# Four layers on one core: layer 2's key-value sums in bursts on two column halves, in place of layer-norm aggregation on GpSimd

## The chip, the core and the metric

The kernel runs on one NeuronCore of a Trainium2 chip. Its engines run side by side and meet through semaphores: PE (TensorE, matrix products; weight loads are shown apart as PEld), DVE (VectorE), ACT (ScalarE), POOL (GpSimd) and SP (SyncE, which here issues DMAs). SBUF is the working memory of 128 partitions; PE writes its results to the eight banks of PSUM. The metric is the device time of one execution in microseconds, the median of the runs.

## What is computed

Two pairs of layers are applied to x of 2048 rows and 512 columns in bf16, each with a layer norm ahead and a residual sum behind. Layers 0 and 2 are linear attention with 32 heads of 16 columns and a Hedgehog feature map; layers 1 and 3 are a gated unit with 1376 hidden columns.

```python
def _A_ref(x, wqkv, w_phi, wo):
    q, k, v = qkv[0], qkv[1], qkv[2]               # 32 heads x 16
    pq = jnp.einsum("bhsd,hdf->bhsf", q, w_phi)
    pk = jnp.einsum("bhsd,hdf->bhsf", k, w_phi)
    phi_q = jnp.concatenate([_softmax(pq, axis=-1), _softmax(-pq, axis=-1)], axis=-1)
    phi_k = jnp.concatenate([_softmax(pk, axis=-1), _softmax(-pk, axis=-1)], axis=-1)
    kv = jnp.einsum("bhsf,bhsd->bhfd", phi_k, v)
    z  = jnp.einsum("bhsf->bhf", phi_k)
    num = jnp.einsum("bhqf,bhfd->bhqd", phi_q, kv)
    den = jnp.einsum("bhqf,bhf->bhq", phi_q, z)[..., None] + 1e-6
    o = num / den
    return (lambda x, *d: x.transpose(*d))(o, 0, 2, 1, 3).reshape(B, S, D) @ wo
...
x = x + _A_ref(_layernorm(x, axis=-1), A_wqkv, A_w_phi, A_wo)
x = x + _B_ref(_layernorm(x, axis=-1), B_W_gate, B_W_up, B_W_down)
x = x + _A_ref(_layernorm(x, axis=-1), A_wqkv, A_w_phi, A_wo)
x = x + _B_ref(_layernorm(x, axis=-1), B_W_gate, B_W_up, B_W_down)
```

The sum over all rows in `kv` and `z` separates the two halves of an attention layer: no output of the layer can be made before the last row's key has been summed.

## The kernel before

x is held in SBUF as 16 tiles of 128 rows (`NT`); four tiles make a slab (`NSLAB`). A column chunk (`NC`, 128 columns) holds eight heads.

Order. Each operation is recorded by `op` or `dma` with the resources that it reads and writes and a planned duration. A planner (`Program.schedule`) then makes the order of each engine's instructions: it runs list schedules over a model of the engines and keeps the one whose replay is shortest. `WINDOW` limits how far each engine may reach ahead. So a change of one operation can move others, and the order in which an engine gets its instructions is fixed when the program is built. DMAs are issued from SP, and a few from ACT.

Layer norm. `ln_stats` makes each tile's statistics with `bn_stats` on DVE (line 551) and, for most tiles, `bn_aggr` on DVE (line 553), then variance plus epsilon (`rv1`, line 558) and the power -1/2 (`rstd`, line 559) on POOL. For tiles 8 to 15 of layer 0, `aggr_pool` (lines 562 to 577) instead takes mean and variance from the two halves in `bn_stats`' output by small POOL operations, for four tiles at a time, and makes rstd and nmr (mean times -rstd) too. `ln` then applies the norm: with rstd and nmr for layer 0's tiles from 4 on, the even ones on DVE (line 592), the odd ones on ACT (line 590); in all other cases on DVE with mean and rstd (line 594). The result goes through a DMA transpose (or, for layer 0's tiles 0 to 3, through PE) into `yT`.

Keys and values. `kv_proj` (one tile) and `kv_pair` (two) make k and v on PE, both exponentials of k (`expk`) and the copy of v (`vsb`) on ACT. `vsb` holds, for each tile and chunk, 128 columns of v and two ones. `knorm` makes the softmax sums on DVE (`Zk`, line 629; their reciprocals `rZk`, line 631) and multiplies `expk` by them in place on POOL (line 634, "phik"); the last two tiles are shared between POOL and DVE. `kv_acc` (line 663) sums, for each tile, eight groups (two signs by four chunks) over the rows: a matmul with 128 stationary columns of `expk` and 129 moving columns of `vsb`, into banks 0 to 2 with three groups to a bank. `kv_fin` multiplies the banks by a block mask into `kvbd` (128 columns of values in an order of d by head, 8 of denominators, 8 of the mask itself, `GW` = 144 in all): lines 674 ("kvbd") and 679 ("kvden"), a pair for each bank.

Queries. `q_proj` makes q transposed, a slab at a time, with its exponentials on ACT (`expq`, line 693). `num` (line 706) multiplies a tile of `expq` by `kvbd`, copies the three banks out (`numcp`), forms the denominators (`zm`, `zd`, `zr`, `ab`), the scaled sum (`tsc`, `o`), transposes it by DMA and multiplies by `wo` (line 737).

Gated unit. `glu_up` (line 758) and `glu_down` (line 785) do the gate, up and down products; `mix` interleaves them with `num` of the layer before and with layer norm, keys and values of the layer after. At the change from layer 1 to layer 2 the order recorded is:

```python
mix(steps_B(tiles(2)), steps_N([14, 15]) + steps_K(0))
mix(steps_B(tiles(3)), steps_K(1) + steps_K(2) + [lambda: self.q_proj(0, mring, "A2")])
for t in range(12):
    self.kv_acc(t, "A2")
for f in steps_K(3):
    f()
for t in tiles(3):
    self.kv_acc(t, "A2")
self.kv_fin("A2")
```

Of the kernel before, what the change touches and what calls it, by code (L numbers as in the profile page):

```python
# [345 lines left out]
FP32 = mybir.dt.float32  # L346
# [4 lines left out]
P = 128  # L351
# [5 lines left out]
NG = 8  # L357
GW = 144
# [10 lines left out]
class Kernel:  # L369
# [27 lines left out]
    def alloc(self, E):  # L397
# [17 lines left out]
        sb("vsb", [NT, NC, 130])  # L415
        sb("expq", [NSLAB, NC, 2, 512])
        sb("kvbd", [NG, GW])
# [9 lines left out]
        sb("mask8t", [8])  # L427
        sb("phi_c", [NC, DH])
# [5 lines left out]
        sb("agg", [4, 3], FP32)  # L434
        sb("aggw", [2], FP32)
# [6 lines left out]
        sb("ab", [2, 64])  # L442
        self.ps = E(nc.psum_tensor("ps", [P, 8, 512], FP32))
# [4 lines left out]
    def setup(self):  # L448
# [46 lines left out]
        op("pool", lambda e: e.memset(k.aggw[:, 0:1], -0.5), [], [r("aggw")], 100, "agg w0")  # L495
        op("pool", lambda e: e.memset(k.aggw[:, 1:2], 1.0 / D), [], [r("aggw")], 100, "agg w1")
        op("pool", lambda e: e.memset(k.vsb[:, :, :, 128:130], 1.0), [], [r("vones")], 250, "v ones")
        op("pool", lambda e: e.tensor_copy(k.kvbd[:, :, 136:144], k.mask8[:].unsqueeze(1).to_broadcast([P, NG, 8])), [r("mask8")], [r("kvones")], 230, "kv ones")
# [33 lines left out]
    def late_weights(self):  # L532
        dma, r, k = self.dma, self.r, self
        pieces = []
        wo_v = self.A_wo.rearrange("(c h d) n -> h d c n", c=4, h=8)
        for h in range(8):
            pieces.append((lambda h: lambda rd: dma("sp", lambda e: e.dma_start(k.wo_p[h:128:8, :, :], wo_v[h]), [rd], [r("wo", h)], 65536, f"dma wo{h}"))(h))
# [9 lines left out]
    def ln_stats(self, ts, tag):  # L547
        op, r, k = self.op, self.r, self
        t0, t1 = ts[0], ts[-1] + 1
        for t in ts:  # L550
            op("dve", (lambda t: lambda e: e.bn_stats(k.stats6[:, t, :], k.x_sb[:, t, :]))(t), [r("x", t)], [r("st", t)], 685, f"{tag} stats {t}")  # L551
            if tag != "L0" or ts[0] < 8:
                op("dve", (lambda t: lambda e: e.bn_aggr(k.mv[:, t, :], k.stats6[:, t, :]))(t), [r("st", t)], [r("mv", t)], 172, f"{tag} aggr {t}")
        if tag == "L0" and ts[0] >= 8:
            return self.aggr_pool(ts, tag)
# [4 lines left out]


    def aggr_pool(self, ts, tag):
        op, r, k = self.op, self.r, self
        t0, t1 = ts[0], ts[-1] + 1
        n = t1 - t0
        s6 = k.stats6[:, t0:t1, :].rearrange("p t (u j) -> p t u j", u=2)
        RS, RV, RR = [r("st", t) for t in ts], [r("rv1", t) for t in ts], [r("rstd", t) for t in ts]
        sm, df = k.agg[:, 0:n, 0:2], k.agg[:, 0:n, 2:3]
        d = 225 + 4 * n
        op("pool", lambda e: e.tensor_tensor(df, s6[:, :, 0, 1:2], s6[:, :, 1, 1:2], ALU.subtract), RS, [r("agg", 1)], d, f"{tag} agdif {t0}")  # L570
        op("pool", lambda e: e.tensor_tensor(sm, s6[:, :, 0, 1:3], s6[:, :, 1, 1:3], ALU.add), RS, [r("agg", 0)], d, f"{tag} agsum {t0}")
        op("pool", lambda e: e.tensor_tensor(df, df, df, ALU.mult), [r("agg", 1)], [r("agg", 1)], d, f"{tag} agsq {t0}")
        op("pool", lambda e: e.tensor_tensor(sm, sm, k.aggw[:].unsqueeze(1).to_broadcast([P, n, 2]), ALU.mult), [r("agg", 0), r("aggw")], [r("agg", 0)], d, f"{tag} agmul {t0}")
        op("pool", lambda e: e.tensor_scalar(df, df, 0.25, EPS_LN, op0=ALU.mult, op1=ALU.add), [r("agg", 1)], [r("agg", 1)], d, f"{tag} agv {t0}")
        op("pool", lambda e: e.tensor_tensor(k.rv1[:, t0:t1, :], df, k.agg[:, 0:n, 1:2], ALU.add), [r("agg", 0), r("agg", 1)], RV, d, f"{tag} rv1 {t0}")
        op("pool", lambda e: e.tensor_tensor(k.rstd[:, t0:t1, :], k.rv1[:, t0:t1, :], k.mhalf[:, 0:n], ALU.pow), RV + [r("mhalf")], RR, 550 + 20 * n, f"{tag} rstd {t0}")  # L576
        op("pool", lambda e: e.tensor_tensor(k.nmr[:, t0:t1, :], k.agg[:, 0:n, 0:1], k.rstd[:, t0:t1, :], ALU.mult), [r("agg", 0)] + RR, [r("nmr", t) for t in ts], d, f"{tag} nmr {t0}")

    def ln(self, t, tag, on_act=False, pe_bank=None, stats=True, copy_act=False):
# [4 lines left out]
        if tag == "L0" and t > 3:  # L584
            if t < 8:
                op("pool", lambda e: e.tensor_scalar(k.nmr[:, t, :], k.mv[:, t, 0:1], k.rstd[:, t, :], -1.0, op0=ALU.mult, op1=ALU.mult), [r("mv", t), r("rstd", t)], [r("nmr", t)], 280, f"{tag} nmr {t}")
            how = ("dve", "act", "pool")[on_act]
            dep, dst = [r("x", t), r("nmr", t), r("rstd", t)], [r("yt", yb)]
            if how == "act":
                op("act", lambda e: e.activation(k.ytile[:, yb, :], k.x_sb[:, t, :], ACT.Identity, scale=k.rstd[:, t, :], bias=k.nmr[:, t, :]), dep, dst, 825, f"{tag} apply {t}")  # L590
            else:
                op(how, lambda e: e.tensor_scalar(k.ytile[:, yb, :], k.x_sb[:, t, :], k.rstd[:, t, :], k.nmr[:, t, :], op0=ALU.mult, op1=ALU.add), dep, dst, 407 if how == "dve" else 2090, f"{tag} apply {t}")
        else:
            op("dve", lambda e: e.tensor_scalar(k.ytile[:, yb, :], k.x_sb[:, t, :], k.mv[:, t, 0:1], k.rstd[:, t, :], op0=ALU.subtract, op1=ALU.mult),
               [r("x", t), r("mv", t), r("rstd", t)], [r("yt", yb)], 407, f"{tag} apply {t}")
# [16 lines left out]
    def kv_proj(self, t, ring, tag):  # L612
# [9 lines left out]
        op("act", lambda e: e.activation(k.vsb[:, t, :, 0:128], k.pb[bv][:].rearrange("p (c n) -> p c n", c=4), ACT.Copy),  # L622
# [18 lines left out]
    def kv_pair(self, t, ring, tag):  # L641
# [11 lines left out]
        op("act", lambda e: e.activation(k.vsb[:, t:t + 2, :, 0:128], k.ps[:, vb[0]:vb[0] + 2, :].rearrange("p b (c n) -> p b c n", c=4), ACT.Copy),  # L653
# [4 lines left out]
    def kv_acc(self, t, tag):  # L658
        op, r, k = self.op, self.r, self
        for g in range(NG):  # L660
# [3 lines left out]
                k.pb[bank][:, j * 130:j * 130 + 129], k.expk[:, t, s, c * 128:(c + 1) * 128], k.vsb[:, t, c, 0:129],  # L664
# [3 lines left out]
    def kv_fin(self, tag):  # L668
        op, r, k = self.op, self.r, self
        for bank in range(3):  # L670
            g0 = bank * 3
            n = min(3, NG - g0)
            pv = k.pb[bank][:, 0:n * 130].rearrange("p (g m) -> p g m", m=130)
            op("dve", (lambda g0, n, pv: lambda e: e.tensor_tensor(
                k.kvbd[:, g0:g0 + n, 0:128].rearrange("p g (d h) -> p g d h", h=8),
                pv[:, :, 0:128].rearrange("p g (h d) -> p g d h", h=8),
                k.mask8[:].unsqueeze(1).unsqueeze(1).to_broadcast([P, n, 16, 8]), ALU.mult))(g0, n, pv),
               [self.RP[bank], r("mask8")], [r("kvbd", bank)], 550 if n == 3 else 430, f"{tag} kvbd {bank}")
            op("dve", (lambda g0, n, pv: lambda e: e.scalar_tensor_tensor(
                k.kvbd[:, g0:g0 + n, 128:136], pv[:, :, 128:129].to_broadcast([P, n, 8]), 0.5 * EPS_DEN,  # L680
                k.mask8[:].unsqueeze(1).to_broadcast([P, n, 8]), ALU.add, ALU.mult))(g0, n, pv),
# [115 lines left out]
    def emit(self):  # L797
# [41 lines left out]
        for li in (0, 2):  # L839
# [51 lines left out]
            if not last:  # L891
                mix(steps_B(tiles(2)), steps_N([14, 15]) + steps_K(0))
                mix(steps_B(tiles(3)), steps_K(1) + steps_K(2) + [lambda: self.q_proj(0, mring, "A2")])
                for t in range(12):
                    self.kv_acc(t, "A2")
                for f in steps_K(3):
                    f()
                for t in tiles(3):
                    self.kv_acc(t, "A2")
# [72 lines left out]
```

## Time and profile before

| | us |
|---|---|
| median of 3 runs | 392.02 |
| lowest and highest run | 391.07, 392.33 |
| the profiled execution | 392.02 |
| its span from the first to the last instruction | 390.3 |

| part of the span | us | what PE does |
|---|---|---|
| layer 0's weights, norm, keys and sums | 0 to 53.7 | waits in part for the other engines |
| first `num` of layer 0 | 53.68 | |
| first gate product of layer 1 | 72.12 | from here nearly without gaps |
| last sums of layer 2 | 237.22 to 239.83 | |
| first `num` of layer 2 | 240.04 | |
| first gate product of layer 3 | 257.82 | |
| last matmul | 378.26 to 387.76 | `glu_down` of the last tiles |

The span is what one execution took from its first to its last instruction; the run's time is 1.7 us longer. A stretch's busy time is summed for each engine. In a list of instructions each line gives the start, the time, the engine, the line of the kernel, the operation with its output and input shapes, and how many equal ones were merged; a bracket gives the idle time ahead of it and who ended it. A matmul's own duration holds the time that it needs to pass through the array, so matmuls overlap; the distance from start to start is what each adds.

### The profile page before, as it was taken

What the parts mean: (1) busy time and instruction counts of PE and PEld (TensorE: products, weight loads), DVE (VectorE), ACT (ScalarE), POOL (GpSimd) and SP (SyncE); (2) the same over time, 40 slices, a digit from 0 to 9 for tenths busy, and PEclk for the clock granted to TensorE, in tenths of its full rate; (3) what the DMA queues carried; (4) which work ended last, traced back from release to release, by engine and by line L of the source; (5) the groups of instructions that cost most, each with busy time, mean ns of one, the idle gap of its engine ahead of it and who ended that gap; (6) DMA issues with size and microseconds to landing.
All of it is one profiled execution on the core that took longest, in us unless ns stands there. A gap on an engine that the chain in (4) does not pass through costs nothing.

```text
span 390.3 us, 6397 instructions
## 1 busy us (share of the span) xinstructions
PE 379.4 (97%) x2331; PEld 208.0 (53%) x2331; DVE 272.0 (70%) x547; ACT 206.6 (53%) x389; POOL 168.5 (43%) x284
## 2 busy tenths in 40 slices
PE   5999989999999999999999999999999999999997
PEld 3445554667644544444444457567774554444444
DVE  4999978877766888866766777897986776232222
ACT  5898859834633404533453484985563462553340
POOL 5499936641724363372244543584553242100000
DMA  6833682311311322401000110132323132100002
GB/s 179 228 67 71 191 299 53 69 40 32 53 40 27 43 55 44 84 10 28 14 15 0 27 29 3 40 80 57 55 55 69 27 42 67 29 14 27 17 12 67
DMA packets 61663, 23.01 MB, mean 59 GB/s; under 512 B 53472, under 2 KB 60608, under 8 KB 61632
## 3 DMA queue, kind: packets, MB, share of 16 engines
q1 hardware_dynamic: 60912, 22.02, 24.4%
q10 hardware_dynamic: 720, 0.59, 0.5%
q8 instruction: 18, 0.29, 0.3%
q14 instruction: 13, 0.11, 0.1%
HBM read 7.91 MB, written 2.10 MB: 26 GB/s over the span
## 4 chain that ended last, share of the span: by engine, by line
PE 88%; POOL 4%; ACT 3%; DMA 2%; DVE 1%; issue 1%; ACTq 0%; POOLq 0%
PE ps L758 39%; PE ps L785 19%; PE ps L617 7%; PE ps L737 7%; PE ps L690 6%; PE ps L706 4%; PE ps L663 3%; PE ps L648 2%; POOL expk L634 2%; ACT expq L693 2%; DVE stats L551 1%; DMA x_sb<-in_A_x_dram 1%; DMA hT<-in_A_wqkv_dram 1%; ACT expk L620 1%; POOL rstd L576 1%
## 5 line engine op out<-in xcount | busy, mean ns | idle before, releaser
L758 PE MATMUL ps<-yT,Wg 128*128 128x512 bf16 (+3 forms) x440 | 130.1, 337 | 0.5 <-DMA yT<-ytile 0.2
L758 PE MATMUL ps<-yT,Wu 128*128 128x512 bf16 (+3 forms) x440 | 129.6, 336 | 0.0
L760 ACT ACTIVATE gate_sb<-ps 128x512 bf16<-128x512 f32 (+3 forms) x110 | 55.9, 512 | 105.3 <-PE ps L758 102.9
L785 PE MATMUL ps<-Wd,hT 128*128 128x512 bf16 (+2 forms) x363 | 106.8, 373 | 0.0
L634 POOL TENSOR_TENSOR expk<-expk,rZk 128x1024 bf16<-128x1024 bf16 (+1 forms) x32 | 59.5, 1878 | 37.1 <-DVE rZk L631 19.7
L758 PEld LDWEIGHTS ps<-yT,Wg 128*128 128x128 bf16 (+1 forms) x440 | 43.4, 100 | 33.8 <-issue 1.1
L758 PEld LDWEIGHTS ps<-yT,Wu 128*128 128x128 bf16 (+1 forms) x440 | 43.7, 100 | 32.6 <-ACT expk L765 0.2
L767 DVE TENSOR_TENSOR hT<-gate_sb,expk 128x512 bf16<-128x512 bf16 (+3 forms) x73 | 29.8, 409 | 37.9 <-ACT expk L765 33.0
L785 PEld LDWEIGHTS ps<-Wd,hT 128*128 128x128 bf16 (+1 forms) x363 | 35.3, 98 | 36.6 <-DVE x_sb L787 0.6
L551 DVE BATCH_NORM_STATS2 stats<-x_sb 128x6 f32<-128x512 bf16 x64 | 42.6, 682 | 5.5 <-DMA x_sb<-in_A_x_dram 5.1
L366 ACT ACTIVATE numbf<-ps 128x432 bf16<-128x432 f32 x64 | 33.1, 536 | 19.5 <-PE ps L706 19.4
L629 DVE TENSOR_REDUCE Zk<-expk 128x64 f32<-128x1024 bf16 x32 | 37.7, 1194 | 5.7 <-ACT expk L620 5.4
L731 POOL TENSOR_TENSOR osb<-tsc 128x512 bf16<-128x512 bf16 x28 | 32.5, 1162 | 19.9 <-DVE tsc L726 17.8
L737 PE MATMUL ps<-wo_p,oT 128*128 128x512 bf16 x128 | 39.8, 379 | 0.0
L770 DVE TENSOR_TENSOR hT<-gate_sb,ps 128x512 bf16<-128x512 bf16 (+2 forms) x37 | 22.7, 613 | 20.8 <-PE ps L758 19.6
L693 ACT ACTIVATE expq<-ps 128x1024 bf16<-128x1024 f32 (+1 forms) x40 | 32.6, 861 | 7.3 <-PE ps L690 7.0
L765 ACT ACTIVATE expk<-ps 128x512 bf16<-128x512 f32 (+3 forms) x73 | 36.1, 497 | 0.1
L706 PE MATMUL ps<-kvbd,expq 128*128 128x144 bf16 x256 | 35.0, 226 | 0.5 <-ACT numbf L366 0.5
L620 ACT ACTIVATE expk<-ps 128x512 bf16<-128x512 f32 x44 | 23.9, 598 | 21.5 <-PE ps L617 21.2
L690 PE MATMUL ps<-yT,Wqp 128*128 128x512 bf16 x128 | 34.6, 379 | 0.6 <-ACT expq L693 0.5
L787 DVE TENSOR_TENSOR x_sb<-x_sb,ps 128x512 bf16<-128x512 bf16 (+1 forms) x33 | 22.0, 669 | 18.8 <-PE ps L785 18.4
L559 POOL TENSOR_TENSOR rstd<-rv,mhalf 128x1 f32<-128x1 f32 (+1 forms) x53 | 31.9, 607 | 2.9
(73 smaller groups left out, 429.2 us busy)
## 6 DMA issues: line engine op xcount, KB each, us to landing
out_dram<-x_sb SPq DMA_DIRECT2D x15, 128.0 KB, 1.7
x_sb<-in_A_x_dram SPq DMA_DIRECT2D x3, 512.0 KB, 6.2
Wu<-in_B_W_up_dram SPq DMA_DIRECT2D x4, 344.0 KB, 5.9
Wg<-in_B_W_gate_dram SPq DMA_DIRECT2D x4, 344.0 KB, 5.5
Wd<-in_B_W_down_dram SPq DMA_DIRECT2D x5, 256.0 KB, 6.9
yT<-ytile SPq DMA_TRANSPOSE x60, 2.5
hT<-in_A_wqkv_dram ACTq DMA_DIRECT2D x4, 128.0 KB, 3.1
x_sb<-in_A_x_dram SPq DMA_DIRECT2D x4, 128.0 KB, 3.7
```

What stands on the lines that cost most here:

```text
L366: return e.activation(out, in_, ACT.Copy) if hasattr(e, "activation") else e.tensor_copy(out, in_)
L551: op("dve", (lambda t: lambda e: e.bn_stats(k.stats6[:, t, :], k.x_sb[:, t, :]))(t), [r("x", t)], [r("st", t)], 685, f"{tag} stats {t}")
L629: op("dve", lambda e: e.tensor_reduce(k.Zk[:, zb, :], k.expk[:, t, :, :].rearrange("p s (h f) -> p (s h) f", f=16), AX.X, ALU.add), [r("ex ...
L634: op(eng, (lambda s0, s1: lambda e: e.tensor_tensor(k.expk[:, t, s0:s1, :].rearrange("p s (h f) -> p (s h) f", f=16), k.expk[:, t, s0:s1, ...
L690: op("pe", (lambda c, ic, bank: lambda e: e.matmul(k.pb[bank][:], k.Wqp[:, ic, c * 128:(c + 1) * 128], k.yT[:, ic, st * 512:(st + 1) * 512 ...
L693: op("act", (lambda c0, s, b0: lambda e: e.activation(k.expq[:, st, c0:c0 + w, s, :], k.ps[:, b0:b0 + w, :], ACT.Exp, scale=(1.0 - 2.0 * s ...
L706: op("pe", (lambda s, c, j, g0, bank: lambda e: e.matmul(k.pb[bank][:, j * GW:(j + 1) * GW], k.expq[:, st, c, s, tt * 128:(tt + 1) * 128], ...
L737: op("pe", (lambda c, bank: lambda e: e.matmul(k.pb[bank][:], k.oT[:, ob, c, :], k.wo_p[:, c, :], start=(c == 0), stop=(c == NC - 1)))(c, ...
L758: op("pe", (lambda bank, W, ic, fc, Mf: lambda e: e.matmul(k.pb[bank][0:Mf, 0:n], W[:, ic, fc * 128:fc * 128 + Mf], k.yT[:, ic, c0:c0 + n] ...
L760: op("act", (lambda Mf, gb, gs: lambda e: e.activation(k.gate_sb[0:Mf, gs, 0:n], k.pb[gb][0:Mf, 0:n], ACT.Relu))(Mf, gb, gs), [self.RP[gb] ...
L765: op("act", (lambda Mf, ub, tu: lambda e: e.activation(k.expk[0:Mf, tu, 0, 0:n], k.pb[ub][0:Mf, 0:n], ACT.Copy))(Mf, ub, tu), [self.RP[ub] ...
L785: op("pe", (lambda fc, Kf, u, c0, bank, m0, m1: lambda e: e.matmul(k.pb[bank][:, m0:m1], k.hT[0:Kf, u, c0:c0 + 128], k.Wd[0:Kf, fc, m0:m1] ...
```

## The change

Two things are exchanged. The first goes back to one way of aggregating statistics: `aggr_pool` and its tiles `agg` and `aggw` are gone, `bn_aggr` on DVE is done for all tiles, POOL makes `rv1` and `rstd`, `nmr` is made only for tiles whose norm ACT applies, and the even tiles of layer 0 are applied on DVE with mean and rstd, as all others are.

The second concerns the sums. `vsb`, `kvbd` and the layout of the sums are split into two halves of four heads each (`u`): 64 columns of values and their own ones, `GH` = 72 columns for each half of `kvbd`. The products in `num`'s tail (`zm`, `ab`, `tsc`) follow this layout, and so do the rows of `wo_p`. Layer 0 keeps `kv_acc`, with 130 moving columns in two runs of 65, and `kv_fin` with the new layout. Layer 2 uses `kv_burst` and `kv_burst_fin`: each group becomes two matmuls with 64 stationary columns and 65 moving columns, one for each half of heads, whose results go to partitions 0 to 63 and 64 to 127 of the same columns of one bank (bank 0 for one sign, bank 1 for the other). Four tiles are recorded as one operation of 64 matmuls; the last slab comes as a burst of three tiles and a burst of one. `kv_burst_fin` waits for the last burst, makes four masked products, adds epsilon to all denominators in one operation (`zt`) and spreads them with the mask in another (`kvden`, which writes all groups). Layer 2's q products of slab 0 are recorded behind the third slab's keys instead of inside the mixed list, with two banks to an exponential (banks 2 and 3).

```diff
-                mix(steps_B(tiles(3)), steps_K(1) + steps_K(2) + [lambda: self.q_proj(0, mring, "A2")])
-                for t in range(12):
-                    self.kv_acc(t, "A2")
+                mix(steps_B(tiles(3)), steps_K(1) + steps_K(2))
+                for ts in [[0, 1, 2, 3], [4, 5, 6, 7], [8, 9, 10, 11]]:
+                    self.kv_burst(ts, "A2")
                 for f in steps_K(3):
                     f()
-                for t in tiles(3):
-                    self.kv_acc(t, "A2")
-                self.kv_fin("A2")
+                self.q_proj(0, cycle([2, 3]), "A2", w=2)
+                for ts in [[12, 13, 14], [15]]:
+                    self.kv_burst(ts, "A2")
+                self.kv_burst_fin("A2")
...
+    def kv_burst(self, ts, tag):
+        r, k = self.r, self
+
+        def acc(e):
+            for t in ts:
+                for s in range(2):
+                    for c in range(NC):
+                        for u in range(2):
+                            last = e.matmul(
+                                k.pb[s][u * 64:u * 64 + 64, c * 65:c * 65 + 65], k.expk[:, t, s, c * 128 + u * 64:c * 128 + u * 64 + 64], k.vsb[:, t, c, u, 0:65],
+                                start=(t == 0 and c == 0), stop=(t == NT - 1), skip_group_check=True)
+            return last
+        self.op("pe", acc, [r("phik", t, s) for t in ts for s in range(2)] + [r("v", t) for t in ts] + [r("vones")], self.RP[0:2],
+                190 + 256 * len(ts), f"{tag} kvacc {ts[0]}")
+
+    def kv_burst_fin(self, tag):
+        op, r, k = self.op, self.r, self
+        m8 = k.mask8[:].rearrange("p (u h) -> p u h", u=2)
+        for s in range(2):
+            pv = k.pb[s][:, 0:260].rearrange("p (g m) -> p g m", m=65)
+            for u in range(2):
+                op("dve", (lambda s, u, pv: lambda e: e.tensor_tensor(
+                    k.kvbd[:, s * 4:s * 4 + 4, u, 0:64].rearrange("p g (d h) -> p g d h", h=4),
+                    pv[:, :, 0:64].rearrange("p g (h d) -> p g d h", h=4),
+                    m8[:, u, :].unsqueeze(1).unsqueeze(1).to_broadcast([P, 4, 16, 4]), ALU.mult))(s, u, pv),
+                   [self.RP[s], r("mask8")] + [r("kvbd", g) for g in range(s * 4, s * 4 + 4)] * u, [r("kvbd", g) for g in range(s * 4, s * 4 + 4)], 420, f"{tag} kvbd {s} {u}")
+        op("dve", lambda e: e.tensor_scalar(k.zt[:].rearrange("p (s g) -> p s g", s=2), k.ps[:, 0:2, 64:260:65], 0.5 * EPS_DEN, None, op0=ALU.add),
+           self.RP[0:2], [r("zt")], 160, f"{tag} zt")
+        op("dve", lambda e: e.tensor_tensor(
+            k.kvbd[:, :, :, 64:68], k.zt[:].unsqueeze(2).unsqueeze(3).to_broadcast([P, NG, 2, 4]),
+            m8.unsqueeze(1).to_broadcast([P, NG, 2, 4]), ALU.mult),
+           [r("zt"), r("mask8")], [r("kvbd", g) for g in range(NG)], 220, f"{tag} kvden")
...
-            if tag != "L0" or ts[0] < 8:
-                op("dve", (lambda t: lambda e: e.bn_aggr(k.mv[:, t, :], k.stats6[:, t, :]))(t), [r("st", t)], [r("mv", t)], 172, f"{tag} aggr {t}")
-        if tag == "L0" and ts[0] >= 8:
-            return self.aggr_pool(ts, tag)
+            op("dve", (lambda t: lambda e: e.bn_aggr(k.mv[:, t, :], k.stats6[:, t, :]))(t), [r("st", t)], [r("mv", t)], 172, f"{tag} aggr {t}")
...
-        if tag == "L0" and t > 3:
-            if t < 8:
-                op("pool", lambda e: e.tensor_scalar(k.nmr[:, t, :], k.mv[:, t, 0:1], k.rstd[:, t, :], -1.0, op0=ALU.mult, op1=ALU.mult), [r("mv", t), r("rstd", t)], [r("nmr", t)], 280, f"{tag} nmr {t}")
-            how = ("dve", "act", "pool")[on_act]
...
+        if on_act:
+            op("pool", lambda e: e.tensor_scalar(k.nmr[:, t, :], k.mv[:, t, 0:1], k.rstd[:, t, :], -1.0, op0=ALU.mult, op1=ALU.mult), [r("mv", t), r("rstd", t)], [r("nmr", t)], 280, f"{tag} nmr {t}")
...
+        row = lambda h: 64 * (h // 4) + h % 4
...
+            pieces.append((lambda h: lambda rd: dma("sp", lambda e: e.dma_start(k.wo_p[row(h):row(h) + 61:4, :, :], wo_v[h]), [rd], [r("wo", h)], 65536, f"dma wo{h}"))(h))
```

## The prediction

> **What bounds the kernel now.** I read the totals first, then the chain that ended last, then busy time by stretch, then the instruction order of the two stretches that the change touches.
>
> ```profile
> PE 379.4 (97%) x2331; PEld 208.0 (53%) x2331; DVE 272.0 (70%) x547; ACT 206.6 (53%) x389; POOL 168.5 (43%) x284
> PE 88%; POOL 4%; ACT 3%; DMA 2%; DVE 1%; issue 1%; ACTq 0%; POOLq 0%
> 20.00:40.00 20.00, 19.69 (x136) 10.50 (x135) 20.00 (x26) 18.11 (x23) 19.75 (x19) 1.00 0.32 67
> 222.00:240.00 18.00, 18.00 (x179) 12.16 (x178) 12.54 (x21) 10.26 (x19) 8.41 (x8) 1.00 0.11 23
> 240.00:260.00 20.00, 19.57 (x136) 10.86 (x136) 17.06 (x43) 18.01 (x28) 10.51 (x22) 1.00 0.23 47
> ```
>
> The columns after a stretch are busy us of PE, weight loads, DVE, ACT and POOL, then the granted clock (1.00 everywhere). From 72 us on PE has almost no gap, so whatever moves the head (0 to 54 us) or the change of layers (222 to 240 us) arrives at the end nearly whole. In the head PE is covered by DVE (20.00 of 20) and POOL (19.75): there the last of the sixteen phik products on POOL sets the end. In 222 to 240 PE itself is full.
>
> ```profile
> 23.06 0.31 DVE L592 TENSOR_SCALAR ytile<-x_sb,rstd,nmr 128x512 bf16<-128x512 bf16 x1
> ...
> 26.41 1.92 DVE L592 TENSOR_SCALAR ytile<-x_sb,rstd,nmr 128x512 bf16<-128x512 bf16 x1
> 28.25 0.54 DVE L631 RECIPROCAL rZk<-Zk 128x64 f32<-128x64 f32 x1
> ```
> ```profile
> 26.25 25.75 POOL L634 TENSOR_TENSOR expk<-expk,rZk 128x1024 bf16<-128x1024 bf16 x14
> ```
>
> POOL runs phik 2 to 15 without a gap from 26.25 to 52.0, 1.88 us a step. The same layer-norm apply takes DVE 0.31 us while POOL does small work, and 1.92 us when it arrives just after POOL has begun a phik: it ends as that phik ends (26.30 + 1.88 = 28.2).
>
> ```profile
> 234.14 1.47 PE L663 MATMUL ps<-vsb,expk 128*128 128x129 bf16 x23
> ...
> 237.22 2.77 PE L663 MATMUL ps<-vsb,expk 128*128 128x129 bf16 x45
> 239.83 0.38 PE L690 MATMUL ps<-yT,Wqp 128*128 128x512 bf16 x1
> 240.04 0.54 PE L706 MATMUL ps<-kvbd,expq 128*128 128x144 bf16 x6
> ```
> ```profile
> 238.70 1.08 DVE L674 TENSOR_TENSOR kvbd<-ps,mask 128x384 bf16<-128x384 f32 x2 [1.43 <-PE ps L663]
> 239.70 0.30 DVE L679 SCALAR_TENSOR_TENSOR kvbd<-ps,mask 128x24 bf16<-128x24 f32 x2
> ```
>
> Forty-five sums in 239.83 - 237.22 = 2.61 us: 58 ns each, 128 of them 7.4 us. DVE masks banks 0 and 1 while PE still sums into bank 2, so layer 2's first `num` starts 0.2 us behind the last sum. That overlap is what the change gives up.
>
> **Part 1, the head.** POOL loses the 2 x 6 small aggregation steps and the two nmr of tiles 4 and 6, and gets rv1 and nmr of single tiles. DVE gets eight bn_aggr. Four of them took 12.92 to 13.20, 0.07 each, so eight add 0.6 us to a DVE that has no gap. By the changed order DVE runs Zk 0, apply 4, four stats, four aggr, four stats, four aggr, rZk 0, Zk 1, apply 6. From Zk 0's end at 14.30: apply 4 waits for rstd (ends 14.74) and is out at 15.1; 8 stats x 0.594 + 8 x 0.07 gives T = 20.5 for the last aggr (rZk 0 started at 19.94 before). POOL then does rv1, rstd (0.09 + 0.30 + 0.98, by the rows at 22.95 and 23.23) and begins phik 0 at T + 1.4 = 21.9. DVE does rZk 0 and Zk 1 (0.46 + 1.10) and reaches apply 6 at T + 1.5. If phik 0 is there first, apply 6 waits to 23.8, as in the row at 26.41; then rZk 1, two Zk, rZk 2 (0.46 + 2.20 + 0.46) put phik 2 at 27.1 to 27.2 in place of 26.3: POOL's end is 0.9 us later. If apply 6 is first, rZk 2 is done at 25.4, before POOL gets to phik 2 (two nmr of 0.27 and two phik behind 21.9: 26.2), and nothing is lost: -0.1. The gap between the two arrivals is 0.1 us, less than I can place, so I take +0.5 and keep -0.1 and +0.9. Behind that, layer 0's sums keep the old form (130 columns for 129), and num follows the last phik through two kvbd and one kvden as before: 0.
>
> **Part 2, layer 2's sums.** Each 129-column matmul becomes two of 65 columns on 64 stationary columns each. The price of one isn't in the trace. Between 512 columns (216 ns apart) and 129 (58) a column costs 0.413 ns, so 65 cost 58 - 64 x 0.413 = 31.6 ns. One end: the halves of a pair run side by side, 128 x 31.6 = 4.0 us. Other end: one after another, 256 x 31.6 = 8.1. Farther: each half needs its own weight load, and the trace shows no load-and-matmul pair faster than 58 ns, 256 x 58 = 14.8. I take 4.0, since the halves share neither array columns nor partitions of the result. Entering and leaving a burst may empty the array: a sum takes 220 ns where they start 58 apart, so 0.16 us of tail; I take one per burst, 5 x 0.16 = 0.8 (ends 0 and 1.6).
>
> The weight loads are the doubt. The trace has 96-column loads (last chunk of Wg and Wu) at 123 ns and 128-column ones at 98: the shorter load is the slower. The Trainium skill, "TensorEngine Tiling (Array Packing)", Restrictions, says that column tiling disables Fast Weight Load, which speaks against this change. By "TensorE: Matmul & The Clock Gate", LDWEIGHTS, a load takes its columns over 1.2 GHz, 53 ns for 64; if the two tiles of a pair load side by side, that is 128 x 53 = 6.8 us in place of 4.0, and the sum below would be +2.3 us, not -0.5; one after another, 13.6 us and about +9. No run here shows which.
>
> **Part 3, when layer 2's num starts.** Before, PE had 113 matmuls of 512 columns and the 128 sums between layer 1's last gate/up matmul and the first num: 24.4 + 7.4 = 31.8 back from 240.04 is 208.2. The changed order has 126, of which one more belongs to q tile 1, so 12 moved behind that point: it comes at 208.2 - 2.6 = 205.6. Ahead of the last burst stand 120 matmuls, four bursts of 15 tiles (15 x 8 x 31.6 ns = 3.8) and 0.6 of switches: 205.6 + 25.9 + 4.4 = 235.9. It needs phik 15. k 15 is done after 106 matmuls and two bursts (2.3): 230.8; before, from k 15's end (233.28) to phik 15's end (236.69 + 1.50) passed 4.9 us, so 235.7: just hidden, by 0.2; faster bursts would gain only through an earlier k 15. The last burst ends at 235.9 + 0.25 + 0.16 switch + 0.16 tail = 236.5. Now nothing is left to sum while DVE makes kvbd: four masks of 256 elements (0.42, the row of that size) and two small ones (0.17) are 2.0 us; num can start at 238.5 instead of 240.04, -1.5. PE fills 1.3 us of it with six q matmuls and stands for 0.7; the rest of slab 1's q and num 1 are queued behind num, and ACT's numcp waits for it. One more q matmul is already done: -0.2. But ACT (18.0 of 20 busy in 240 to 260) now makes the two expq of q columns 2 and 3 (1.04 each) only after the last burst: from 237.4 to 239.5, with numcp 0 behind them, which began at 240.43 before. So ACT's chain gains 0.9, not 1.7. I take -1.0, since ACT is the fuller engine there; ends -1.8 and, with slow halves, far above 0.
>
> **Part 4, at nothing.** tsc, zm, ab and kvbd run in inner runs of 4 for 8 with the same elements; DVE has 391 - 272 us free. If tsc went from 0.69 to the 1.4 ns an element of the kvbd row, 0.8 us would show in the first tiles of each layer, at most +1.5 in all. The wo DMAs keep 8 issues of 64 KB on SP; the last is issued near 42.9 and lands 2.3 us later, and PE reads wo first at 62.0: 17 us of cover. Two memsets less and a mask copy more on POOL lie in its wait for phi_c (1.3 us).
>
> **Sum.** +0.5 - 1.0 = -0.5 us against the span of 390.3, which was profiled at 392.02, the median of the three runs (391.07 to 392.33): 391.5. What a measurement of this kernel can tell from no change is about 0.3%, 1.2 us.
>
> **Rivals.** *Slower, one mechanism:* the halves of a pair don't overlap. 8.1 for 4.0 us puts num at 242.6, +2.4 with the q matmul, +0.5 head: 394.9. For it: no tiled matmul in the trace, and every half has its own load. Against: disjoint columns and results. Taking 128 pairs, the sum is 0 at +0.5 us or 36 ns a pair, and slower by 0.3% from 45 ns a pair. *Faster:* switches cost nothing and apply 6 slips in ahead of phik 0: then phik 15 (about 235.4) sets the last burst, num at 237.8, ACT's chain -1.7, head -0.1: 390.2. *It does not do what it says:* bursts are fast, but phik 15 comes late on POOL behind DVE's queue (margin 0.2), each us late coming back whole, plus the head's 0.9: 392.5 when 0.6 late.
>
> **Chances.** Forecast 0.60, within it 0.17 faster by over 0.3%, 0.38 same, 0.05 slower (the late phik 15 is in it; its own range 390.4 to 392.7). Faster rival 0.17. Slower rival 0.23. So 0.34, 0.38, 0.28. The range goes from the faster rival, 390.0, to the slower one, 395.0; the 14.8 us end stays out.
>
> **What would show it.** Head: apply 6 at about 1.8 us or 0.3, phik 2's start at 27.2 or 26.3, layer 0's first num at 53.7 to 54.6. Bursts: 32 ns a pair or 63. Layer 2: a PE gap of 0.5 to 1 us ended by DVE's kvden ahead of num, num near 238.5 plus the head's shift. It is wrong if a burst of four tiles takes over 1.5 us, if the gap ahead of num is over 1.5, or if PE shows new gaps between 72 and 205 us or after 260.

## The result and the profile after

The changed kernel takes 394.91 us, the median of 4 runs (394.30 to 395.15), against 391.80 (391.07 to 392.33) for the kernel before beside it: a ratio of 1.0078, with a 95% interval of 1.0057 to 1.0099. A second measurement of the same instructions, below, gave 1.0060 (1.0045 to 1.0075). The change makes the kernel slower by some 0.6 to 0.8%, about 2.5 to 3 us. I had forecast 391.5, in a range from 390.0 to 395.0.

The page's chain by engine, of the kernel after:

```profile
PE 77%; DVE 11%; POOL 4%; DMA 4%; issue 2%; ACT 1%; SPq 0%; POOLq 0%; DVEq 0%
```

DVE holds 11% of the chain that sets the end, where it held 1% before. The same three stretches as before, after the change (columns as there):

```profile
20.00:40.00 20.00, 18.80 (x129) 9.98 (x127) 19.32 (x29) 18.18 (x25) 18.58 (x13) 1.00 0.40 77
222.00:240.00 18.00, 16.98 (x311) 9.21 (x310) 15.66 (x20) 10.29 (x18) 11.38 (x8) 1.00 0.08 17
240.00:260.00 20.00, 18.40 (x120) 9.41 (x119) 15.83 (x40) 18.32 (x27) 8.28 (x18) 1.00 0.17 35
```

In the head DVE and POOL, full before, stand 0.7 and 1.4 us. At the change of layers PE, which had no gap, stands 1.0 us, and behind it 1.6 in place of 0.4. So the sums did get shorter, and PE now waits in their place. Four instants, read from PE's order of instructions, say where the 3 us of the trace arise:

| us | before | after | difference of the step |
|---|---|---|---|
| layer 0's first num | 53.68 | 55.21 | +1.53 |
| layer 1's first gate matmul | 72.12 | 73.36 | -0.29 |
| layer 2's first num | 240.04 | 241.85 | +0.57 |
| end of the last matmul | 387.76 | 390.83 | +1.26 |

These add up to 3.07, against 3.0 between the spans (393.3 and 390.3). By the forecast the last two together should have come out at -1.0; they came out at +1.83. The last step is the least certain: from layer 2's first num to the last matmul this trace takes 148.98 us and a second one of the same instructions 148.73, while three traces with layer 2 in the order of before (the kernel before and two runs below) take 147.72 to 148.37.

**Head.** DVE's order, then POOL's, of the kernel after:

```profile
21.75 2.05 DVE L569 TENSOR_SCALAR ytile<-x_sb,mv,rstd 128x512 bf16<-128x512 bf16 x1
...
26.85 0.31 DVE L569 TENSOR_SCALAR ytile<-x_sb,mv,rstd 128x512 bf16<-128x512 bf16 x1
...
38.95 1.22 DVE L604 TENSOR_REDUCE Zk<-expk 128x64 f32<-128x1024 bf16 x1 [0.68 <-ACT expk L626]
...
43.22 1.22 DVE L604 TENSOR_REDUCE Zk<-expk 128x64 f32<-128x1024 bf16 x1 [1.10 <-ACT expk L626]
```
```profile
21.73 1.93 POOL L609 TENSOR_TENSOR expk<-expk,rZk 128x1024 bf16<-128x1024 bf16 x1
...
27.00 13.40 POOL L609 TENSOR_TENSOR expk<-expk,rZk 128x1024 bf16<-128x1024 bf16 x7 [0.66 <-DVE rZk L606]
40.71 3.81 POOL L609 TENSOR_TENSOR expk<-expk,rZk 128x1024 bf16<-128x1024 bf16 x2 [0.30 <-DVE rZk L606]
44.97 1.93 POOL L609 TENSOR_TENSOR expk<-expk,rZk 128x1024 bf16<-128x1024 bf16 x1 [0.45 <-DVE rZk L606]
```

POOL begins phik 0 at 21.73, DVE gets to apply 6 at 21.75 and is held until phik 0 is over. That costs POOL 0.66 us ahead of phik 2. Apply 8 follows at 26.85 (23.06 before), so its k and its exponential come 3.3 us later, the later exponentials too, and twice DVE waits for one and POOL for DVE.

**Change of layers.** DVE's order of the kernel after, with POOL's of the same stretch below:

```profile
218.51 1.60 DVE L569 TENSOR_SCALAR ytile<-x_sb,mv,rstd 128x512 bf16<-128x512 bf16 x1
...
223.09 1.76 DVE L569 TENSOR_SCALAR ytile<-x_sb,mv,rstd 128x512 bf16<-128x512 bf16 x1
...
227.72 1.94 DVE L569 TENSOR_SCALAR ytile<-x_sb,mv,rstd 128x512 bf16<-128x512 bf16 x1 [0.56 <-POOL rstd L557]
...
235.80 1.21 DVE L604 TENSOR_REDUCE Zk<-expk 128x64 f32<-128x1024 bf16 x1
```
```profile
218.04 1.93 POOL L609 TENSOR_TENSOR expk<-expk,rZk 128x1024 bf16<-128x1024 bf16 x1
...
222.77 1.93 POOL L609 TENSOR_TENSOR expk<-expk,rZk 128x1024 bf16<-128x1024 bf16 x1 [0.89 <-DVE rZk L606]
...
227.58 1.93 POOL L609 TENSOR_TENSOR expk<-expk,rZk 128x1024 bf16<-128x1024 bf16 x1
231.52 5.27 POOL L609 TENSOR_TENSOR expk<-expk,rZk 128x1024 bf16<-128x1024 bf16 x3 [2.01 <-DVE rZk L606]
237.74 1.49 POOL L609 TENSOR_TENSOR expk<-expk,rZk 128x512 bf16<-128x512 bf16 x1 [0.95 <-DVE rZk L606]
```

It is the meeting of the head three times over: applies 13, 14 and 15 come to DVE 0.47, 0.32 and 0.14 us after POOL has begun a phik, and each ends about 0.15 us behind the end of that phik. The last one ends at 229.66; from there DVE runs Zk 12 to 15 and what belongs to them with hardly a pause, and phik 15 follows on POOL at 237.74. The exponential that Zk 15 reads was done at 234.30, as ACT's order shows:

```profile
233.21 1.09 ACT L595 ACTIVATE expk<-ps 128x512 bf16<-128x512 f32 x2 [1.09 <-PE ps L592]
```

PE's order of the same stretch; the row at 232.13 is k 15:

```profile
222.99 1.20 PE L669 MATMUL ps<-vsb,expk 128*64 128x65 bf16 x64
224.12 1.04 PE L592 MATMUL ps<-Wkp,yT 128*128 128x512 bf16 x4
...
232.13 1.04 PE L592 MATMUL ps<-Wkp,yT 128*128 128x512 bf16 x4
...
236.94 0.95 PE L669 MATMUL ps<-vsb,expk 128*64 128x65 bf16 x48 [0.37 <-POOL expk L609]
237.82 1.04 PE L700 MATMUL ps<-yT,Wqp 128*128 128x512 bf16 x4
239.38 0.44 PE L669 MATMUL ps<-vsb,expk 128*64 128x65 bf16 x16 [0.52 <-POOL expk L609]
239.75 1.04 PE L700 MATMUL ps<-yT,Wqp 128*128 128x512 bf16 x4
241.41 0.60 PE L700 MATMUL ps<-yT,Wqp 128*128 128x512 bf16 x2 [0.61 <-DVE zt L687]
241.85 0.54 PE L716 MATMUL ps<-kvbd,expq 128*128 128x144 bf16 x6
```

The bursts are as fast as hoped: 64 half matmuls take 1.13 us from start to the next instruction, 48 take 0.88, 16 take 0.37. All five make 4.6 us, in place of 7.4 for the 128 sums before. But the last two wait for POOL, and the two q matmuls ahead of num wait for the masks, since their banks 0 and 1 still hold the sums.

**Behind num.** ACT's order of the kernel after; before, the first `numcp` (the copy of num's banks) began at 240.43, 0.39 us behind num:

```profile
240.83 1.94 ACT L703 ACTIVATE expq<-ps 128x1024 bf16<-128x1024 f32 x2 [3.63 <-PE ps L700]
242.65 0.96 ACT L367 ACTIVATE numbf<-ps 128x432 bf16<-128x432 f32 x2
```

The two exponentials of q columns 2 and 3 take both columns at once and can be made only behind the last burst, since the last four of their eight matmuls stand there on PE. The first numcp comes 0.80 us behind num.

### The profile page after: what moved, and what is told of

Read it like the earlier page. It is cut to its first block, busy times and chain, and to the rows that moved or that the text cites. A ratio compares the mean times of both kernels' runs of the same rounds, so it can differ in the third digit from the quotient of the medians.

```text
span 393.3 us, 6628 instructions
## 1 busy us (share of the span) xinstructions
PE 379.2 (96%) x2459; PEld 204.6 (52%) x2459; DVE 272.5 (69%) x555; ACT 206.2 (52%) x385; POOL 167.5 (43%) x273
## 4 chain that ended last, share of the span: by engine, by line
PE 77%; DVE 11%; POOL 4%; DMA 4%; issue 2%; ACT 1%; SPq 0%; POOLq 0%; DVEq 0%
PE ps L768 37%; PE ps L795 19%; PE ps L747 6%; PE ps L592 5%; PE ps L700 4%; PE ps L716 4%; POOL expk L609 3%; DVE ytile L569 2%; DVE Zk L604 2%; DVE stats L552 2%; DMA oT<-osb 2%; PE ps L623 2%; DVE rZk L606 1%; DMA x_sb<-in_A_x_dram 1%; DMA yT<-ytile 1%
## 5 line engine op out<-in xcount | busy, mean ns | idle before, releaser
L768 PE MATMUL ps<-yT,Wg 128*128 128x512 bf16 (+3 forms) x440 | 127.6, 336 | 0.8 <-DMA yT<-ytile 0.4
L768 PE MATMUL ps<-yT,Wu 128*128 128x512 bf16 (+3 forms) x440 | 124.7, 337 | 0.0
L795 PE MATMUL ps<-Wd,hT 128*128 128x512 bf16 (+2 forms) x363 | 105.2, 373 | 0.0
L747 PE MATMUL ps<-wo_p,oT 128*128 128x512 bf16 x128 | 40.8, 379 | 1.2 <-DMA oT<-osb 1.1
L556 POOL TENSOR_SCALAR rv<-mv 128x1 f32<-128x1 f32 (+1 forms) x55 | 12.5, 230 | 64.1 <-DVE mv L553 63.9
L569 DVE TENSOR_SCALAR ytile<-x_sb,mv,rstd 128x512 bf16<-128x512 bf16 x58 | 31.3, 544 | 6.6 <-POOL rstd L557 6.1
L703 ACT ACTIVATE expq<-ps 128x1024 bf16<-128x1024 f32 (+1 forms) x36 | 31.8, 946 | 7.3 <-PE ps L700 7.2
```

Source lines behind the costliest of these rows:

```text
L747: op("pe", (lambda c, bank: lambda e: e.matmul(k.pb[bank][:], k.oT[:, ob, c, :], k.wo_p[:, c, :], start=(c == 0), stop=(c == NC - 1)))(c, ...
L768: op("pe", (lambda bank, W, ic, fc, Mf: lambda e: e.matmul(k.pb[bank][0:Mf, 0:n], W[:, ic, fc * 128:fc * 128 + Mf], k.yT[:, ic, c0:c0 + n] ...
L795: op("pe", (lambda fc, Kf, u, c0, bank, m0, m1: lambda e: e.matmul(k.pb[bank][:, m0:m1], k.hT[0:Kf, u, c0:c0 + 128], k.Wd[0:Kf, fc, m0:m1] ...
```

## The experiments

In all of them the planner is replaced by a fixed list of instructions for each engine, taken from the plan of before or after, so that nothing moves but what the text names. Each time is a median beside runs of the kernel before (392.00 to 392.22 in these sets); the ratio to before is the safer number.

**The kernel after again.** No edit.

> Kernel after once more, unedited (its instructions and their order are the same), beside the next three, so that they are compared on one chip. Expected 394.4 to 395.3 us, 0.6 to 0.9% above before, and in the trace the same places: layer 0's first num near 55.2, 186.5 us from there to layer 2's first num, 19.3 us from that to the first gate matmul of layer 3.

394.72 us, ratio 1.0060 (1.0045 to 1.0075); num at 55.10 and 186.63 behind it. The trace repeats to 0.4 us. Over all runs with this head, layer 0's first num lies between 54.64 and 55.62, so a single trace places the head to some 0.5 us.

**The old head.** The three functions of before (`ln_stats`, `aggr_pool`, `ln`), and before's order on every engine up to layer 0's last mask.

```diff
-            op("dve", (lambda t: lambda e: e.bn_aggr(k.mv[:, t, :], k.stats6[:, t, :]))(t), [r("st", t)], [r("mv", t)], 172, f"{tag} aggr {t}")
+            if tag != "L0" or ts[0] < 8:
+                op("dve", (lambda t: lambda e: e.bn_aggr(k.mv[:, t, :], k.stats6[:, t, :]))(t), [r("st", t)], [r("mv", t)], 172, f"{tag} aggr {t}")
+        if tag == "L0" and ts[0] >= 8:
+            return self.aggr_pool(ts, tag)
```

> Kernel after, with the head of before: mean and variance of tiles 8 to 15 on POOL again and the head's work in the order of before on every engine; from layer 0's first num on everything is as after. Theory A (the loss has two places, about 1.2 us in the head and about 2 us at the change of layers): layer 0's first num at 53.7 us of the span in place of 55.21, the time 1.2 to 1.5 us below after, 393.4 to 393.8 us, and still above before. Rival B (the head's delay is taken up later, all of the loss is in layer 2's sums): num at 53.7 too, but the time within 0.4 us of after, 394.5 to 395.3. Rival C (all of the loss is in the head): the time of before, about 391.8.

393.20 us, ratio 1.0028 (1.0020 to 1.0037); first num at 53.56. About 0.3% comes back (the median lies 0.2 us below theory A's range), and not all of the loss: B and C fall.

**The new head on the kernel before.** The mirror of that edit.

> The mirror of the run with the old head: kernel before, with bn_aggr on DVE for all tiles and the head in the order of after; layout, sums and order behind the head are those of before. Theory A: first num of layer 0 near 55.2 us, the time 1.2 to 1.5 us above before, 393.0 to 393.3. Rival B: within 0.4 us of before, 391.4 to 392.2. Rival C: the whole loss, 394.5 to 395.

392.71 us, ratio 1.0026 (1.0015 to 1.0038), and first num at 55.41. The ratio makes it 1.0 us; the median is 0.3 below the range that I gave. The head alone costs 1.0 to 1.5 us.

**The new aggregation in the old order.** Kernel after; only the order of the head changes. DVE's, from the last statistics on:

```diff
-aggr 12..15, rZk 0, Zk 1, apply 6, rZk 1, Zk 2, Zk 3, rZk 2, apply 8, rZk 3
+aggr 12..15, apply 6, rZk 0, Zk 1, Zk 2, rZk 1, apply 8, rZk 2, Zk 3, Zk 4, rZk 3
```

> Kernel after, aggregation on DVE as in after, but the head's work in the order of before on SP, ACT, PE and DVE: apply 6 ahead of the first reciprocal (so before POOL begins phik 0), apply 8 ahead of rZk 2; the four bn_aggr stand behind their four bn_stats. If the loss of the head is the meeting of apply 6 with phik 0 and the late apply 8 (theory A's mechanism): apply 6 takes 0.3 us, not 2.05, phik 2 begins at 26.2 in place of 27.00, the first num at 53.9 to 54.2 in place of 55.21, the time 0.9 to 1.3 us below after: 393.6 to 394.0. If it is the longer DVE work itself (eight bn_aggr) that costs: apply 6 short, but phik 2 at 26.8 or later and the time within 0.4 us of after.

DVE's applies 6 and 8, then POOL's phik 0 and phik 1 to 4, in this run:

```profile
19.27 0.38 DVE L569 TENSOR_SCALAR ytile<-x_sb,mv,rstd 128x512 bf16<-128x512 bf16 x1
...
22.68 0.31 DVE L569 TENSOR_SCALAR ytile<-x_sb,mv,rstd 128x512 bf16<-128x512 bf16 x1
```
```profile
20.81 1.93 POOL L609 TENSOR_TENSOR expk<-expk,rZk 128x1024 bf16<-128x1024 bf16 x1
...
23.32 7.63 POOL L609 TENSOR_TENSOR expk<-expk,rZk 128x1024 bf16<-128x1024 bf16 x4
```

392.99 us, ratio 1.0026 (1.0012 to 1.0040), first num at 52.78, both better than I had expected. All of the head's loss is gone with the same eight bn_aggr on DVE; POOL runs from phik 1 on without a gap and starts phik 2 at about 25.2, a us ahead of before's 26.25. The head's loss came from the order that the planner made, not from the work that moved to DVE. This run takes the old order on PE, DVE, ACT and SP at once, so it doesn't part apply 6 from apply 8.

**The applies let through.** Kernel after, its order unchanged; POOL begins phik 9, 10 and 11 only behind the apply that it held up.

```diff
-    AFTER = []
+    AFTER = [('A2 phik 9 0', 'L2 apply 13'), ('A2 phik 10 0', 'L2 apply 14'), ('A2 phik 11 0', 'L2 apply 15')]
```

> Kernel after with its order on every engine unchanged; the only edit is that POOL begins phik 9, 10 and 11 of layer 2 only when apply 13, 14 and 15 are done on DVE. Theory A: the three applies take 0.4 us each in place of 1.60, 1.76 and 1.94; apply 15 ends near 227 us in place of 229.66; the chain Zk 12 to 15, then phik 15, ends 1 to 1.5 us earlier (near 238 in place of 239.23), PE's waits of 0.28, 0.37 and 0.52 us ahead of k 15 and the last two bursts shrink to 0.3 in sum, and layer 2's first num comes 0.8 to 1.1 us earlier relative to layer 0's first num; time 393.8 to 394.1. Rival: PE's own work or the mask chain behind the last burst sets num, not phik 15: num moves by less than 0.3 us and the time stays within 0.4 us of after.

DVE's last apply, POOL's phik 15 and PE's last two bursts in this run:

```profile
225.70 0.41 DVE L569 TENSOR_SCALAR ytile<-x_sb,mv,rstd 128x512 bf16<-128x512 bf16 x1 [0.57 <-POOL rstd L557]
```
```profile
236.02 1.50 POOL L609 TENSOR_TENSOR expk<-expk,rZk 128x512 bf16<-128x512 bf16 x1 [0.94 <-DVE rZk L606]
```
```profile
236.18 0.95 PE L669 MATMUL ps<-vsb,expk 128*64 128x65 bf16 x48
238.03 0.44 PE L669 MATMUL ps<-vsb,expk 128*64 128x65 bf16 x16
```

393.25 us, ratio 1.0030 (1.0018 to 1.0042): 0.3% or 1.2 us below after, the median 0.5 us below the range that I had given. Apply 15 is done at 226.11 (229.66 in after), phik 15 at 237.52 (239.23), no burst waits, and num lies 185.10 us behind layer 0's first num, in place of 186.64: 1.5 us earlier, more than I had expected. POOL loses nothing by waiting 0.9, 0.8 and 0.6 us there; it had them to spare.

**Behind num, the order of before.** ACT's, for one:

```diff
-numcp 0 0, numcp 0 1, expq 1 0 0, numcp 1 0, numcp 1 1, expq 1 0 1
+numcp 0 0, numcp 0 1, numcp 1 0, numcp 1 1, expq 1 0 0, expq 1 0 1
```

> Kernel after up to layer 2's first num; from there on the order of before on every engine (numcp 0 and 1 ahead of the first expq of slab 1 on ACT, fewer q matmuls between num 0 and num 1 on PE). Before takes 17.78 us from layer 2's first num to the first gate matmul of layer 3, after 19.27, with the same operations. If the 1.5 us between them are the planner's order of that stretch (expq 1 0 ahead of numcp 1): 17.8 to 18.4 us, time 0.9 to 1.4 us below after. If they are the two late expq of q columns 2 and 3 and the q matmuls that wait for zt: 18.8 to 19.3 us, time within 0.5 us of after.

394.47 us, ratio 1.0052 (1.0039 to 1.0064), which is not told apart from after. The first gate matmul does come at 18.21 us behind num, but from there to the last matmul it is 130.43 us for 129.45: my mark was bad, since the gate matmul only changed places with other PE work. From num to the end of the last matmul it is 148.64, in after 148.73 and 148.98. So the order behind num alone gives nothing that can be measured.

**Other banks.** Six q matmuls of slab 1, not two, also stand ahead of num.

```diff
-                self.q_proj(0, cycle([2, 3]), "A2", w=2)
+                self.q_proj(0, cycle([2, 3, 4, 5]), "A2", w=2)
...
-            qring, gring, dring = cycle([0, 1, 2, 3]), cycle([0, 1, 2, 3]), wring
+            qring, gring, dring = cycle([2, 3, 0, 1] if li else [0, 1, 2, 3]), cycle([2, 3, 0, 1] if li else [0, 1, 2, 3]), wring
```

> Kernel after with other banks only: q columns 2 and 3 of slab 0 in banks 4 and 5, slab 1's q from bank 2 on, layer 3's gate ring from bank 2 on too, and six q matmuls of slab 1 (two before) ahead of layer 2's first num, where PE stood 0.61 us for zt. If PE is what the stretch behind the sums waits for: no PE wait ahead of num, four more q matmuls done there, time 0.6 to 0.9 us below after. If ACT is (expq of q columns 2 and 3, then numcp 0 and 1, back to back from 240.8 us on): the wait vanishes and comes back as PE waits behind num, numcp 0 begins within 0.2 us of its place in after, time within 0.3 us of after (394.4 to 395.0).

394.88 us, ratio 1.0073 (1.0054 to 1.0091): no gain. The wait for zt is gone, and PE waits behind num instead, for ACT (PE's order of this run):

```profile
243.91 0.30 PE L716 MATMUL ps<-kvbd,expq 128*128 128x144 bf16 x2 [0.79 <-ACT numbf L367]
```

**Three mends at the change of layers.** The waits of the gated run, the banks (all but the gate's) and the order of before behind num.

> Kernel after with the head left as it is and all three mends at the change of layers: phik 9, 10, 11 begin behind apply 13, 14, 15; q columns 2 and 3 of slab 0 go to banks 4 and 5 and slab 1's q to banks 2 and 3, six of its matmuls ahead of the first num, so that none waits for the masks to leave banks 0 and 1; behind the first num the order of before. Theory: no PE wait ahead of that num (0.61 in after, 0.62 in the gated run), num 185.0 to 185.5 us behind layer 0's, 17.3 to 17.9 us from num to the first gate matmul of layer 3; time 2.5 to 3.3 us below after and 0.2 to 1.2 below before's. Rival (ACT is the bound of the stretch and takes back what PE gains): num as said but 18.8 or more to the gate matmul, time 1.5 to 2 us below after, as the gated run alone.

393.57 us, ratio 1.0033 (1.0022 to 1.0043). Num lies 185.17 us behind layer 0's, as said, and no more comes of it than in the gated run, as the rival has it; but the time is only 1.1 us below after by the ratios, short of the rival's 1.5 to 2. Part of that is my own edit, which left the gate's ring at bank 0, where slab 3's last q columns now lay:

```profile
259.20 0.27 PE L768 MATMUL ps<-yT,Wg 128*128 128x256 bf16 x1 [1.49 <-ACT expq L703]
```

**q ahead of the bursts, alone.** Kernel after with the banks above, the order of before behind num, and the place of eight q matmuls:

```diff
-v 15, burst 12-14, 4 of q columns 2 and 3, burst 15, 4 of q columns 2 and 3, 2 of slab 1, num 0
+v 15, 8 of q columns 2 and 3, burst 12-14, burst 15, 6 of slab 1, num 0
```

> Kernel after with its own head and with nothing done about the applies that wait behind POOL; the only mend is the place of q columns 2 and 3 of slab 0: all eight matmuls ahead of the fourth burst (in banks 4 and 5, slab 1's q and layer 3's gate from bank 2 on), so that both expq are made before the last sum, and the order of before behind num. If the two late expq on ACT are what costs after its 0.7 to 1.2 us between layer 2's first num and the end: PE's waits of 0.37 and 0.52 us ahead of the last bursts shrink, num within 0.3 us of its place in after, numcp 0 begins 0.4 us behind num in place of 0.8, num to the last matmul 147.6 to 148.0 us in place of 148.7 to 149.0, time 0.8 to 1.2 us below after, 393.5 to 394.0. If the bank change alone is what matters (it gave nothing by itself) or the stretch is bound elsewhere: within 0.4 us of after.

ACT's order in this run:

```profile
238.67 1.94 ACT L703 ACTIVATE expq<-ps 128x1024 bf16<-128x1024 f32 x2 [1.13 <-PE ps L700]
242.41 0.95 ACT L367 ACTIVATE numbf<-ps 128x432 bf16<-128x432 f32 x2 [1.80 <-PE ps L716]
```

393.86 us, ratio 1.0040 (1.0025 to 1.0054), 0.2% or 0.8 us below after. Num stays (186.66 us behind layer 0's), ACT now waits for PE ahead of numcp, which begins 0.40 us behind num, and num to the last matmul takes 148.10 us. Neither the banks nor the order alone gave anything, so the place of the two exponentials is the likely cause. It is not shown: the interval overlaps that of after (1.0045 to 1.0075) and that of the run with before's order behind num (1.0039 to 1.0064), and the two runs at the end, which differ in this place and in two q matmuls of slab 1, can't be told apart either.

**The layout alone.** Kernel before with the sums, masks and tail in head halves; against the kernel after, besides the old head and before's order:

```diff
-                for ts in [[0, 1, 2, 3], [4, 5, 6, 7], [8, 9, 10, 11]]:
-                    self.kv_burst(ts, "A2")
+                for t in range(12):
+                    self.kv_acc(t, "A2")
...
-                self.kv_burst_fin("A2")
+                self.kv_fin("A2")
```

> Kernel before in everything but the layout: sums of 130 columns in head halves in both layers, masks, tail products and rows of wo by halves; the head, the order and layer 2's sums tile by tile are those of before. If the tail in halves costs nothing, as the prediction has it: time within 0.4 us of before, 391.5 to 392.4, and 17.8 us from layer 2's first num to the first gate matmul. If the products in inner runs of four cost (tsc 1.4 us for 0.69): 18.5 us or more there, 19 or more behind layer 0's, time 0.8 to 1.6 us above before.

391.98 us, ratio 0.9993 (0.9982 to 1.0005), 17.84 us to the gate matmul. The layout costs nothing.

**All mends together, in two forms.** New aggregation in the old order, the gated applies, the banks with the gate's ring mended, the order of before behind num; in the second form q columns 2 and 3 also stand ahead of the last two bursts.

> All mends together: the head of the run with the new aggregation in the old order; phik 9 to 11 behind apply 13 to 15; the banks of the run beside it (so that layer 3's first gate matmul doesn't wait 1.49 us for an expq, as it did in the run with three mends); four q matmuls of slab 1 ahead of num; behind num the order of before. Expected from the parts: layer 0's first num at 52.8 us, layer 2's 184.9 to 185.4 behind it, 17.8 to 18.3 us to the first gate matmul; time 389.8 to 391.0, 0.3 to 0.5% below before. If the gains at the change of layers are taken back by ACT behind num: 390.8 to 391.8, no better than before by 0.3%.

> As the run with all mends, but all eight q matmuls of columns 2 and 3 stand ahead of the fourth burst, so that their two expq are made before the last sum, and six q matmuls of slab 1 fill PE while DVE masks. If late expq on ACT is what holds the stretch behind num: numcp 0 begins 0.4 us behind num in place of 0.8 or more, num itself 0.6 to 0.9 us later than in the run beside it, and the time 0.2 to 0.6 us below that run. If not: the later num comes back whole, the time is 0.3 to 0.9 us above that run.

The first takes 391.29 us, ratio 0.9983 (0.9969 to 0.9998), the second 391.19, ratio 0.9974 (0.9959 to 0.9989). Both beat the kernel before; the first lies in the range that I had given for gains taken back behind num (390.8 to 391.8). In the traces the second has num 0.42 us later behind layer 0's, and 147.59 for 148.68 us from num to the last matmul; the times of the two can't be told apart, and the difference of 0.1 us is in neither of the ranges that I had given. With its losses undone the change is worth about 0.2% (the two intervals together go from 0.0 to 0.4%), where the sums alone are 2.8 us (0.7%) shorter on PE.

## Why the prediction was wrong

**Right.** The price of a half matmul: (1.13 - 0.37) / 48 = 15.8 ns, 31.7 a pair, where I took 31.6; what is left for entering and leaving a burst is 0.37 - 16 x 0.0158 = 0.12 us, where I took 0.16. The rival of halves that don't overlap falls; that its 394.9 us is what was measured is luck. The tail behind the last burst: 2.1 us from its end (239.75) to num, forecast 2.0. Part 4, the layout at nothing.

**The head: right mechanism, too small.** "The gap between the two arrivals is 0.1 us, less than I can place, so I take +0.5 and keep -0.1 and +0.9." The gap was 0.02 us, the block came, and phik 2 began at 27.00 for the 27.1 to 27.2 that I gave for it. The end of the bracket was wrong: first num came 1.5 us late, not 0.9. I followed the block only through the reciprocals to POOL. In the same queue stood apply 8, moved by the planner from 23.06 to 26.85, and from it went transpose, k, exponential and Zk, another 1.78 us of waits on DVE and 0.75 on POOL.

**The failed step: "just hidden, by 0.2".** I put k 15 at 230.8 and from its end to phik 15's end the 4.9 us of before. Measured, less the 1.24 us that layer 1 began late: k 15 ends at 231.75, and the way from there to phik 15's end takes 6.2 us (232.99 to 239.23). So phik 15 was not hidden: it ended 2.1 us behind the 235.9 at which I had the last burst begin. The 4.9 held for a DVE that had nothing waiting; here DVE came to Zk 15 at 235.80, 1.5 us behind its exponential (done at 234.30), after applies held for 1.60, 1.76 and 1.94 us. I had shown that very row in the head, and had not applied it to the layer-norm applies of layer 2, which before were held once (1.23 us) and after three times. The gated run shows it: without the three blocks the way from k 15's end (232.69) to phik 15's end (237.52) is 4.8 us, no burst waits and 1.2 us come back. Half of k 15's own delay of 0.95 us stays there, so that part isn't the applies. So what happened is the rival that I called "it does not do what it says", at 2.2 us late (the last burst at 239.38, less 1.24, for the 235.9 that I had), not 0.6; and as it said, that came back whole at num (241.85 less the same 1.24 is 240.61, for 238.5).

**The sized term: "I take -1.0" for ACT's chain.** I had seen that the two expq stand behind the last burst, and priced it as a smaller gain (0.9 for 1.7). That was counted against a num at 238.5. With num late all the same, nothing of the gain was left, and num to the end got longer, by 0.4 to 1.3 us depending on the traces compared (148.7 to 149.0 for 147.7 to 148.4); the run with q ahead of the bursts gives back 0.8 us, though not clear of noise. The wait of slab 1's q for zt I had not foreseen, and the run with other banks shows that it cost nothing.

**Sum.** Against the second measurement of after, the mended places are worth 1.2 to 1.4 us (head), 1.2 (applies) and 0.8 (expq, uncertain), some 3.3 in all; all together gave 0.9974 for 1.0060, which is 3.4 us. Of the 2.8 us that PE's sums save, 1.3 reach num in the gated run (185.10 behind layer 0's for 186.36 before), since the masks that ran beside the sums now stand behind them, 2.1 us from the last burst's end to num. What stays open is why the complete mend keeps only about 1 us, with a head that is itself 0.3 to 0.9 us ahead of before's (first num at 52.77 to 53.36); that ACT, 18.4 of 20 us busy behind num in that kernel too, takes the rest was argued, not tried.

## What to carry to other kernels

Where a planner orders the work, an edit that removes operations from one engine is also an edit of every queue; price the new order row by row, each instruction that is known to be held up by another engine's long one above all. A burst that needs the last tile gains only what the chain to that tile gains: before making the sums faster, follow the last tile from its norm to its product, with the queue that each link stands in. When a mark in the middle moves, look at the end too: here a gate matmul came 1 us sooner, and the end stayed.

## What the runs showed of the hardware

Matmuls of 65 columns that go to the two column halves in turn start 15.8 ns apart, 31.7 a pair: as long as I had estimated for one of them alone (31.6), and a little over half of the 58 ns of a full one of 129 columns, though each has its own weight load. So the two of a pair overlap. Such a load takes 111 ns, longer than the 98 of a full 128-column load, but the 64 loads of a burst pass in 1.09 us, so they overlap too. The Trainium skill, "TensorEngine Tiling (Array Packing)", Restrictions, rules out Fast Weight Load with column tiling; that may be in the longer load, which no run here shows, but it set no time here, and the 53 ns a load that I had estimated from "TensorE: Matmul & The Clock Gate", LDWEIGHTS, would have made the sums 6.8 us in place of 4.6.

The same layer-norm apply takes 0.31 or 0.41 us, and 1.60 to 2.05 when POOL has begun a phik up to 0.5 us earlier (it ends about 0.15 us behind that phik), while DVE's Zk of twice the elements takes about 1.2 at any time. The Trainium skill, "SBUF — State Buffer", Who interferes with whom, fits this: a `tensor_scalar` in a two-port mode and a GpSimd instruction lock each other out for a whole instruction, and a `tensor_reduce` never does; that the apply runs in such a mode no row here says. Letting the short one go first cost POOL 0.6 to 0.9 us of waiting each time and saved DVE 1.2 to 1.5.
